# Retention and a gated MLP in one kernel: float32 scores from paired q and k, the state in 64x64 corners of the array, one pinned burst

## The chip, the cores and the metric

The kernel runs on one core of one Trainium2 chip. The metric is device time of one execution in microseconds. Its engines are named as in the profile: PE is TensorE (matmul), PEld its weight loads, DVE is VectorE, ACT is ScalarE, POOL is GpSimd, SP issues the DMAs. SBUF is the working memory; PE writes to PSUM, eight banks of 2 KB per partition, which DVE and ACT read.

## The reference

Inputs are q, k and v of shape (8, 8, 576, 64): batch B, head H, position S, head width D. First comes a retention layer per head, then a gated MLP with a spatial gate, per batch.

```python
scores = scale * np.matmul(q, k.transpose(0, 1, 3, 2))      # scale = 1/sqrt(D)
gamma = 1.0 - 2.0 ** (-5.0 - np.arange(H))
Dmat = np.where(rel >= 0, gamma[:, None, None] ** rel[None], 0.0)   # rel = pos_row - pos_col
attn = np.matmul(scores * Dmat[None], v)
x = attn.transpose(0, 2, 1, 3).reshape(B, S, H * D)          # (8, 576, 512)
h = np.maximum(x @ w_in, 0.0)                                # w_in is float64, 512 x 1024
u, v = h[..., :512], h[..., 512:]
v_n = (v - mean(v)) / np.sqrt(var(v) + 1e-06)                # over the last axis
v_s = np.einsum('ts,bsd->btd', w_spatial, v_n) + b_spatial[None, :, None]
out = (u * v_s) @ w_out                                      # w_out is float64, 512 x 512
```

## The kernel before

**Retention** works in chunks of 128 positions, four and a tail of 64 per batch (`NC`, `TL`). Inside a chunk the masked scores are formed directly. What earlier chunks contribute comes from a state of 64x64 per head: `state(c)` adds kᵀv of the chunk to the decayed state, `outp(c)` multiplies the state with the decayed q (`qsc`, line 283) and adds the masked scores times v (line 286). The sum `xo` is split into a rounded high part and a low remainder (lines 290, 291), because the MLP's matmuls run in float32r, three to a product (`mm3`, lines 316 to 318).

Two heads share the 128 partitions in most tiles: head 2p on rows 0 to 63, head 2p+1 on rows 64 to 127. The state is kept block-diagonal, 128x128 per pair of heads, and the blocks off the diagonal are zero.

**Scores** exist in two forms. Batch 0 (`DIRECT = 1`) uses `scores_direct`: float32 matmuls of depth 64, even heads on the upper half of the array's rows and odd heads on the lower half. Batches 1 to 7 use `split_qk` and `scores`: q and k come twice over the partitions (`qk`), ACT and DVE split them into high and low parts (lines 225 to 228), one float32r matmul of depth 128 per head and 256 columns gives two partial sums (line 241), ACT copies one out (243), DVE adds the other (244) and POOL applies the mask (245). `prep(c)` scales k by `kd` (256) and q by `qs` (259) on POOL.

**The MLP** of a batch is `v_block` (five, one per chunk), then in `main` eight `u` tiles, eight `vs` tiles (the spatial gate) and eight `f` tiles (the output), each followed by its work on ACT and DVE. Batch 0's v blocks are traced beside its retention; later v blocks are in `main`.

**What sets the order.** The code is traced in one order and a planner reorders it, by the traced order as priority and by simulated times; afterwards each engine runs its list in order, with semaphore waits. `interleave` mixes `main(b)` with `retention(b + 1)`: each `yield` carries a weight, and whichever side is behind its share (`ta`, `tr`) is traced next. `keep_in_program_order` ties an instruction to the one traced just before it on the same engine; before the change only the DMAs of the start are tied so. `issue_after` holds the conversion of w_spatial and w_out behind a mark. At the start the float64 weights are converted with integer arithmetic on DVE (`from_f64`, lines 166 to 170 and 160), eight quarters of w_in (`w_half`), then w_out (`w_o`). The loads of `qk` lie in a pool `late`, which is opened where the weights' staging pool `sp` was.

**PSUM**: two banks for scores (`ps_sc`), one each for `ds` and `xo` (`ps_x`), four for the MLP (`ps_m`).

Of the kernel before, what the change touches and what calls it, by code (L numbers as in the profile page):

```python
# [10 lines left out]
F32 = mybir.dt.float32  # L11
# [21 lines left out]
DIRECT = 1  # L33
# [3 lines left out]
def retention_gmlp(ctx, tc, kvq, kp, qk, qk_t, qp_t, kp_t, v_t, w_in, w_sp, b_sp, w_out, amask, qscale, kdec, sdec, out):  # L37
# [10 lines left out]
    am = cp.tile([P, H, C], F32, name="am")  # L48
# [12 lines left out]
    st = [cp.tile([P, NP, P], F32, name=f"st{i}") for i in range(3)]  # L61
    late = []
# [9 lines left out]
    low = cp.tile([P, 1], F32, name="low")  # L72
    nc.vector.memset(low[:D], 0.0)
    nc.vector.memset(low[D:], -1.0)

# [14 lines left out]
    def load_k(b, c):  # L90
        n = C if c < NC else TL
        if b < DIRECT:
            t = wk.tile([P, NP, C], F32, name=f"kp_{b}_{c}", tag="ks")
            dma(t[:, :, :n], kp[b, c] if c < NC else kp_t[b])
            return t, None
        t = late[0].tile([P, 2, H, C], F32, name=f"qk_{b}_{c}", tag="qk", bufs=2)
        dma(t[:, :, :, :n], qk[b, c] if c < NC else qk_t[b])
        return t[:, 0], t[:, 1]

    def load_v(b, c):  # L100
        t = ld.tile([P, 3, 512], F32, name=f"kvq_{b}_{c}", tag="kvq")
        qp = t[:, 0].rearrange("p (a n) -> p a n", a=NP)
        if c < NC:
            dma(t, kvq[b, c])
        else:
            dma(qp[:, :, :TL], qp_t[b])
            dma(t[:TL, 2], v_t[b])
        return qp, t[:, 1], t[:, 2]

    def load(b, c):  # L110
        chunk[b, c] = load_k(b, c) + load_v(b, c)
# [30 lines left out]
    k00 = load_k(0, 0)  # L142
    v00 = load_v(0, 0)
    chunk[0, 0] = k00 + v00
    dma(am, amask)
# [4 lines left out]
    k01 = load_k(0, 1)  # L150
    fetch_win(1, 2)
    chunk[0, 1] = k01 + load_v(0, 1)
    fetch_win(1, 3)
    for t in st:
        nc.gpsimd.memset(t, 0.0)
# [23 lines left out]
    def w_o():  # L179
        for db in range(NDB):  # L180
            from_f64(wout[0][:, db], wout[1][:, db], staged["o", db], wk.tile([P, DM], F32, name=f"f_o{db}", tag="ks"))
# [13 lines left out]

    def retention(b, then=None):
        at = {}
        qsc = {}
        ready = {}

        def scores_direct(c):
            n = C if c < NC else TL
            k, _, q, _, _ = chunk[b, c]
            ps = [ps_sc.tile([P, 4, C], F32, name=f"sc_{b}_{c}_{i}", tag="sc") for i in range(2)]
            for h in range(H):
                i, p = h % 2, h // 2
                r = slice(i * D, (i + 1) * D)
                nc.tensor.matmul(ps[i][:n, p, :n], k[r, p, :n], q[r, p, :n], start=True, stop=True)
                if h == 3:
                    yield 0.9  # L210
            a = [wk.tile([P, 4, C], F32, name=f"at_{b}_{c}_{i}", tag="at", bufs=4) for i in range(2)]
            for i in range(2):
                nc.vector.tensor_tensor(out=a[i][:n, :, :n], in0=ps[i][:n, :, :n], in1=am[:n, i::2, :n], op=ALU.mult)
            at[c] = [a[h % 2][:, h // 2] for h in range(H)]
            yield 0.9

        def split_qk(c):
            n = C if c < NC else TL
            q, k, _, _, _ = chunk[b, c]
            ready[c] = []  # L220
            for hf in range(2):
                qh = wk.tile([P, 4, 2, C], F32R, name=f"qh_{b}_{c}_{hf}", tag="qh")
                ks = wk.tile([P, 4, C], F32R, name=f"ks_{b}_{c}_{hf}", tag="ks")
                hs = slice(4 * hf, 4 * hf + 4)
                nc.scalar.copy(out=ks[:, :, :n], in_=k[:, hs, :n])  # L225
                nc.vector.scalar_tensor_tensor(out=ks[:, :, :n], in0=ks[:, :, :n].bitcast(F32), scalar=low, in1=k[:, hs, :n], op0=ALU.mult, op1=ALU.add)  # L226
                nc.scalar.copy(out=qh[:, :, 0, :n], in_=q[:, hs, :n])
                nc.vector.tensor_tensor(out=qh[:, :, 1, :n], in0=q[:, hs, :n], in1=qh[:, :, 0, :n].bitcast(F32), op=ALU.subtract)  # L228
                ready[c].append((qh, ks))

        def scores(c):
            at[c] = []
            n = C if c < NC else TL
            for hf in range(2):
                qh, ks = ready[c][hf]
                hs = slice(4 * hf, 4 * hf + 4)
                a = wk.tile([P, 4, C], F32, name=f"at_{b}_{c}_{hf}", tag="at", bufs=4)
                for p in range(2):
                    ps = ps_sc.tile([P, 2, 2, C], F32, name=f"sc_{b}_{c}_{hf}_{p}", tag="sc")
                    for i in range(2):  # L240
                        nc.tensor.matmul(ps[:n, i, :, :n], ks[:, 2 * p + i, :n], qh[:, 2 * p + i, :, :n], start=True, stop=True)  # L241
                    t = late[0].tile([P, 2, C], F32, name=f"a2_{b}_{c}_{hf}_{p}", tag="a2", bufs=2)
                    nc.scalar.copy(out=t[:n, :, :n], in_=ps[:n, :, 1, :n])  # L243
                    nc.vector.tensor_tensor(out=a[:n, 2 * p:2 * p + 2, :n], in0=ps[:n, :, 0, :n], in1=t[:n, :, :n], op=ALU.add)  # L244
                nc.gpsimd.tensor_tensor(out=a[:n, :, :n], in0=a[:n, :, :n], in1=am[:n, hs, :n], op=ALU.mult)  # L245
                at[c] += [a[:, h] for h in range(4)]
                yield 0.48

        def prep(c):
            _, _, q, kn, _ = chunk[b, c]  # L250
            n = C if c < NC else TL
            if b >= DIRECT:
                split_qk(c)
# [8 lines left out]
        def state(c):  # L262
            _, _, _, kn, vv = chunk[b, c]
            ps = ps_x.tile([P, NP, D], F32, name=f"ds_{b}_{c}", tag="ds")
            for h in range(H):
                nc.tensor.matmul(ps[h % 2 * D:(h % 2 + 1) * D, h // 2, :], kn[:, h * D:(h + 1) * D], vv[:, h * D:(h + 1) * D], start=True, stop=True)  # L266
            new = st[(c + 1) % 2]
            for i in range(2):
                r = slice(i * D, (i + 1) * D)
                if c == 0:  # L270
                    nc.scalar.copy(out=new[r, :, r], in_=ps[r])
                else:
                    nc.vector.tensor_tensor(out=new[r, :, r], in0=ps[r], in1=st[2][r, :, r], op=ALU.add)
            if c + 1 < NC:
                nc.gpsimd.tensor_tensor(out=st[2], in0=new, in1=sd.broadcast_to([P, NP, P]), op=ALU.mult)

        def outp(c):
            n = C if c < NC else TL
            vv = chunk[b, c][4]
            ps = ps_x.tile([P, NP, C], F32, name=f"xo_{b}_{c}", tag="xo")  # L280
            if c > 0:
                for p in range(NP):
                    nc.tensor.matmul(ps[:, p, :n], st[c % 2][:, p, :], qsc[c][:, p, :n], start=(p == 0), stop=False)  # L283
            for h in range(H):
                p, i = h // 2, h % 2
                nc.tensor.matmul(ps[i * D:(i + 1) * D, p, :n], vv[:n, h * D:(h + 1) * D], at[c][h][:n, :n],  # L286
                                 start=(c == 0), stop=(c == 0 or p == NP - 1))
            t = slice(c * C, c * C + n)
            hi, lo = (xs[b][:, i, :, t] if c < NC else xt[:, :, i] for i in range(2))
            nc.scalar.copy(out=hi, in_=ps[:, :, :n])  # L290
            mark["x", b, c] = nc.vector.tensor_tensor(out=lo, in0=ps[:, :, :n], in1=hi.bitcast(F32), op=ALU.subtract).ins  # L291
# [5 lines left out]
        if b >= DIRECT:  # L297
            for c in range(2):
# [129 lines left out]
    for step, _ in enumerate(retention(0, more)):  # L428
        if step < 4:
            next(wv)  # L430
# [83 lines left out]
```

## Time and profile before

| | |
|---|---|
| median of three runs | 622.74 us (622.13 to 623.81) |
| the profiled execution, its own time | 622.56 us |
| its span, first to last instruction | 620.8 us |
| busy: PE, DVE, ACT, POOL | 594.9, 433.5, 311.2, 212.0 us |
| mean granted TensorE clock | 0.973 of full |
| moved by DMA | 80.25 MB, 129 GB/s on average |

How to read the rows that follow. A timeline row has the start in us from the span's start, the length in us, the engine, the line of the kernel, the operation, what it writes and reads, the tile of the array (rows*columns), the shapes and the number of records merged into the row; in brackets the idle time before it and what ended that. A group row has shapes and count, then busy us and the mean ns of one, then the engine's idle time before and its releaser. Busy time counts overlapping records once. A float32 matmul is recorded as two matmuls, a float32r one as a single one.

### The profile page before, as it was taken

The page shows a single profiled execution, that of the slowest core. Times are in us where ns is not written, and L with a number is a line of the kernel's source. Part 1 is how long each engine was busy: PE and PEld are TensorE (multiplying, and loading weights), DVE is VectorE, ACT ScalarE, POOL GpSimd, SP SyncE. Part 2 cuts the span into 40 slices and gives each one's busy share as a digit, 9 for nine tenths or more (in the row PEclk, how much of TensorE's full clock was granted, in tenths as well). Part 3 has the DMA queues.
Part 4 walks back from the last instruction along what each step waited for, and adds up shares of the span by engine and source line. Part 5 has one row for each costly group of instructions (what it writes and reads, how often), then busy time and mean ns, then how long its engine had stood idle before and what let it go on. Part 6 is the DMA issues. An engine that isn't in the chain of part 4 may idle for free.

```text
span 620.8 us, 11999 instructions
## 1 busy us (share of the span) xinstructions
PE 594.9 (96%) x4660; PEld 537.3 (87%) x4660; DVE 433.5 (70%) x865; ACT 311.2 (50%) x736; POOL 212.0 (34%) x174
## 2 busy tenths in 40 slices
PE   6977968999999999999999999999999999999997
PEld 4666957887999889997999889997899979998997
DVE  4998798769854796749965697747956598634440
ACT  2346564357633574346633585346733477234522
POOL 2524024526512544224532355214531345310000
PEclk8888977999999999999999999999999999999999
DMA  8735725473324435155324434155333533010002
GB/s 308 251 98 165 262 73 177 168 259 120 94 77 169 146 121 168 61 176 197 87 86 150 165 119 110 62 177 200 104 124 112 185 137 86 18 49 30 1 1 77
DMA packets 42971, 80.25 MB, mean 129 GB/s; under 512 B 22049, under 2 KB 32289, under 8 KB 39330
## 3 DMA queue, kind: packets, MB, share of 16 engines
q1 hardware_dynamic: 42914, 79.49, 38.2%
q8 instruction: 36, 0.59, 0.4%
q14 instruction: 21, 0.17, 0.1%
HBM read 70.03 MB, written 9.44 MB: 128 GB/s over the span
## 4 chain that ended last, share of the span: by engine, by line
PE 86%; DVE 7%; DMA 3%; issue 1%; ACT 1%; SPq 0%; POOL 0%; ACTq 0%; DVEq 0%; POOLq 0%
PE xo L286 6%; PE f L316 6%; PE vs L316 6%; PE u L316 6%; PE f L318 5%; PE f L317 5%; PE vs L317 5%; PE vs L318 5%; PE sc L241 5%; PE v L316 5%; PE u L317 5%; PE u L318 5%; PE v L318 5%; PE v L317 4%; PE xo L283 4%; PE ds L266 3%
## 5 line engine op out<-in xcount | busy, mean ns | idle before, releaser
L245 POOL TENSOR_TENSOR at<-at,am 128x512 f32<-128x512 f32 (+1 forms) x70 | 100.3, 1433 | 122.1 <-DVE at L244 120.4
L228 DVE TENSOR_TENSOR qh<-qk,qh 128x512 fp32r<-128x512 f32 (+1 forms) x70 | 94.1, 1344 | 0.0
L244 DVE TENSOR_TENSOR at<-sc,a 128x256 f32<-128x256 f32 (+1 forms) x140 | 49.9, 388 | 59.9 <-ACT a L243 59.0
L256 POOL TENSOR_TENSOR kvq<-kvq,kd 128x512 f32<-128x512 f32 x32 | 37.2, 1164 | 141.2 <-DMA kvq<-in_kvq 115.8
L316 PE MATMUL u<-x,win 128*128 128x288 f32 x256 | 79.2, 309 | 0.0
L316 PE MATMUL f<-g,wout 128*128 128x288 f32 x256 | 77.7, 303 | 0.0
L316 PE MATMUL vs<-wsp,vn 128*128 128x288 f32 x256 | 77.4, 302 | 0.0
L317 PE MATMUL vs<-wsp,vn 128*128 128x288 f32 x256 | 75.9, 297 | 0.0
L317 PE MATMUL u<-x,win 128*128 128x288 f32 x256 | 75.9, 297 | 0.0
L318 PE MATMUL vs<-wsp,vn 128*128 128x288 f32 x256 | 75.9, 297 | 0.0
L318 PE MATMUL u<-x,win 128*128 128x288 f32 x256 | 75.8, 296 | 0.0
L386 ACT CAST g<-vs 128x288 fp32r<-128x288 f32 x64 | 25.4, 403 | 100.6 <-DVE vs L385 100.6
L317 PE MATMUL f<-g,wout 128*128 128x288 f32 x256 | 75.7, 296 | 0.0
L318 PE MATMUL f<-g,wout 128*128 128x288 f32 x256 | 75.7, 296 | 0.0
L226 DVE SCALAR_TENSOR_TENSOR ks<-ks,low,qk 128x512 fp32r<-128x512 f32 (+1 forms) x70 | 63.4, 905 | 3.0 <-ACT ks L225 2.2
L396 ACT COPY o<-f 128x288 f32<-128x288 f32 x64 | 25.6, 400 | 70.3 <-PE f L318 67.1
L318 PE MATMUL v<-win,x 128*128 128x512 f32 x128 | 52.5, 410 | 3.7 <-DVE x L291 3.7
L316 PE MATMUL v<-win,x 128*128 128x512 f32 x128 | 53.6, 420 | 2.1 <-ACT x L290 2.1
L243 ACT COPY a<-sc 128x256 f32<-128x256 f32 (+1 forms) x140 | 43.9, 356 | 18.5 <-PE sc L241 17.2
L259 POOL TENSOR_TENSOR qsc<-kvq,qs 128x512 f32<-128x512 f32 (+1 forms) x32 | 41.1, 1284 | 33.6 <-DMA kvq<-in_qp_t 33.6
L317 PE MATMUL v<-win,x 128*128 128x512 f32 x128 | 51.6, 403 | 0.0
L286 PE MATMUL xo<-at,kvq 128*64 128x128 f32 (+1 forms) x640 | 49.2, 281 | 2.5 <-POOL at L245 1.6
(92 smaller groups left out, 1407.3 us busy)
## 6 DMA issues: line engine op xcount, KB each, us to landing
qk<-in_qk SPq DMA_DIRECT2D x28, 1024.0 KB, 4.9
kvq<-in_kvq SPq DMA_DIRECT2D x32, 768.0 KB, 5.4
out<-o SPq DMA_DIRECT2D x64, 144.0 KB, 2.0
raw_i<-in_w_in SPq DMA_DIRECT2D x8, 512.0 KB, 5.5
qk<-in_qk_t SPq DMA_DIRECT2D x7, 512.0 KB, 4.5
raw_o<-in_w_out SPq DMA_DIRECT2D x4, 512.0 KB, 4.2
wl_s<-in_w_sp SPq DMA_DIRECT2D x4, 288.0 KB, 2.8
kp<-in_kp SPq DMA_DIRECT2D x4, 256.0 KB, 5.8
```

Of the source, the lines that this page charges most:

```text
L226: nc.vector.scalar_tensor_tensor(out=ks[:, :, :n], in0=ks[:, :, :n].bitcast(F32), scalar=low, in1=k[:, hs, :n], op0=ALU.mult, op1=ALU.add)
L228: nc.vector.tensor_tensor(out=qh[:, :, 1, :n], in0=q[:, hs, :n], in1=qh[:, :, 0, :n].bitcast(F32), op=ALU.subtract)
L241: nc.tensor.matmul(ps[:n, i, :, :n], ks[:, 2 * p + i, :n], qh[:, 2 * p + i, :, :n], start=True, stop=True)
L243: nc.scalar.copy(out=t[:n, :, :n], in_=ps[:n, :, 1, :n])
L244: nc.vector.tensor_tensor(out=a[:n, 2 * p:2 * p + 2, :n], in0=ps[:n, :, 0, :n], in1=t[:n, :, :n], op=ALU.add)
L245: nc.gpsimd.tensor_tensor(out=a[:n, :, :n], in0=a[:n, :, :n], in1=am[:n, hs, :n], op=ALU.mult)
L256: nc.gpsimd.tensor_tensor(out=kh, in0=kh, in1=kd.broadcast_to([P, H, D]), op=ALU.mult)
L259: nc.gpsimd.tensor_tensor(out=t[:, :, :n], in0=q[:, :, :n], in1=qs[:, :, :n], op=ALU.mult)
L286: nc.tensor.matmul(ps[i * D:(i + 1) * D, p, :n], vv[:n, h * D:(h + 1) * D], at[c][h][:n, :n], start=(c == 0), stop=(c == 0 or p == NP - 1))
L316: nc.tensor.matmul(ps, w[0], r[0], start=start, stop=False)
L317: nc.tensor.matmul(ps, w[0], r[1], start=False, stop=False)
L318: nc.tensor.matmul(ps, w[1], r[0], start=False, stop=stop)
```

## The change

All batches form their scores directly in float32 from paired q and k. One transfer per chunk, `qkv`, holds q and k as pairs of heads, k by position, and v (four times 512 values per partition); `qk`, `kp`, `qp_t`, `kp_t`, `split_qk`, the old `scores` and the pool `late` are gone, and the mask is one DVE multiplication of 128x1024 from PSUM.

`state` and `outp` become `burst`. For the state update each head's kᵀv is cut into two halves of 64 positions, so that 16 float32 matmuls of 64x64 go to the four corners of the array, into two banks (one per row half), and DVE adds the two banks and the decayed state in two steps. The state is held as 64x64 per head, with no zero blocks, and the decayed state's part of the output is 8 matmuls in the four corners. In odd pairs the heads swap column halves, which changes the order of x's features; the rows of w_in are permuted on the host to match. The values' matmuls keep depth 128 and 64 columns; in the tail they go to the corners as well.

The helper `mm` ties every retention matmul to the PE instruction traced before it. A chunk is now traced as: `prep(c + 1)`, the burst of c, the load of c + 2, then the scores of c + 1, with new weights for `yield` and `tr`. Scores and bursts share a PSUM tag of two tiles with two banks each. w_out's staging moves from the tag `qh` to the tag `raw` of the staging pool, the conversion's scratch likewise; there are four o buffers instead of three, and the weight conversion of w_in's v half is driven by two steps of two quarters instead of four steps of one.

```diff
-DIRECT = 1
...
-    ps_sc = ctx.enter_context(tc.tile_pool(name="ps_sc", bufs=2, space=PSUM))
-    ps_x = ctx.enter_context(tc.tile_pool(name="ps_x", bufs=1, space=PSUM))
+    ps_r = ctx.enter_context(tc.tile_pool(name="ps_r", bufs=2, space=PSUM))
...
-    st = [cp.tile([P, NP, P], F32, name=f"st{i}") for i in range(3)]
-    late = []
+    st = [cp.tile([P, NP, D], F32, name=f"st{i}") for i in range(3)]
...
+    def load(b, c):
+        t = ld.tile([P, 4, 512], F32, name=f"qkv_{b}_{c}", tag="qkv")
+        q, k = (t[:, i].rearrange("p (a n) -> p a n", a=NP) for i in range(2))
...
+        elif (b, c) == (0, 0):
+            dma(t[:, :2], qkv[b, c, :, :2])
+            dma(am, amask)
+            dma(t[:, 3], qkv[b, c, :, 3])
+            dma(t[:, 2], qkv[b, c, :, 2])
         else:
+            dma(t, qkv[b, c])
+        chunk[b, c] = q, k, t[:, 2], t[:, 3]
...
     def fetch_wout(db):
-        t = wk.tile([P, DM], U64, name=f"raw_o{db}", tag="qh")
+        t = sp.tile([P, DM], U64, name=f"raw_o{db}", tag="raw", bufs=3)
...
+    def mm(out, w, r, start, stop):
+        tc.keep_in_program_order(nc.tensor.matmul(out, w, r, start=start, stop=stop))
...
         def scores(c):
+            n = rows(c)
+            q, k, _, _ = chunk[b, c]
+            ps = ps_r.tile([P, 2, NP, C], F32, name=f"sc_{b}_{c}", tag="r")
+            for p in range(NP):
+                for i in range(2):
+                    mm(ps[:n, i, p, :n] if c < NC else ps[half[i], i, p, :n], k[half[i], p, :n], q[half[i], p, :n], True, True)
+            a = wk.tile([P, 2, NP, C], F32, name=f"at_{b}_{c}", tag="at")
+            if c < NC:
+                nc.vector.tensor_tensor(out=a, in0=ps, in1=am, op=ALU.mult)
...
+        def burst(c):
+            n = rows(c)
+            _, _, kn, vv = chunk[b, c]
+            ps = ps_r.tile([P, 2, 2, 2 * C], F32, name=f"ox_{b}_{c}", tag="r")
+            ds = ps[:, :, 0].rearrange("p r (a d) -> p r a d", a=NP)
+            xo = ps[:, :, 1].rearrange("p j (a n) -> p j a n", a=2)
+            if c < NC:
+                for p in range(NP):
+                    for r in range(2):
+                        for i in range(2):
+                            m = i ^ r
+                            hd = slice((2 * p + m) * D, (2 * p + m + 1) * D)
+                            mm(ds[half[m], r, p], kn[half[r], hd], vv[half[r], hd], True, True)
+            order = [(p, i) for j in range(2) for p, i in ((2 * j, 0), (2 * j, 1), (2 * j + 1, 1), (2 * j + 1, 0))]
+            if c > 0:
+                for p, i in order:
+                    mm(xo[half[i ^ (p % 2)], i, p // 2, :n], st[c % 2][half[i], p], qsc[c][half[i], p, :n], p < 2, False)
+            for p, i in order:
+                h = 2 * p + i
+                r = slice(0, n) if c < NC else half[i]
+                mm(xo[half[i ^ (p % 2)], i, p // 2, :n], vv[r, h * D:(h + 1) * D], at[c][r, i, p, :n], c == 0, c == 0 or p >= 2)
...
+            if c < NC:
+                new, tmp = st[(c + 1) % 2], st[2]
                 if c == 0:
+                    nc.scalar.copy(out=tmp, in_=ds[:, 0])
                 else:
+                    nc.vector.tensor_tensor(out=tmp, in0=ds[:, 0], in1=tmp, op=ALU.add)
+                nc.vector.tensor_tensor(out=new, in0=ds[:, 1], in1=tmp, op=ALU.add)
+                if c + 1 < NC:
+                    nc.gpsimd.tensor_tensor(out=tmp, in0=new, in1=sd.broadcast_to([P, NP, D]), op=ALU.mult)
+            nc.scalar.copy(out=hi, in_=src)
+            mark["x", b, c] = nc.vector.tensor_tensor(out=lo, in0=src, in1=hi.bitcast(F32), op=ALU.subtract).ins
...
         prep(0)
+        scores(0)
+        yield 0.95
         for c in range(NC + 1):
             if then:
                 then(c)
             if c < NC:
                 prep(c + 1)
+            burst(c)
+            if c + 2 < len(nxt) and nxt[c + 2][0] < B:
                 load(*nxt[c + 2])
+            yield 1.7
+            if c < NC:
+                scores(c + 1)
+                yield 0.95
...
-        if step < 4:
+        if step < 2:
+            next(wv)
             next(wv)
...
-        interleave(main(b, b == 0), retention(b + 1) if b + 1 < B else [], 50.0 if b else 38.0, 15.4)
+        interleave(main(b, b == 0), retention(b + 1) if b + 1 < B else [], 50.0 if b else 38.0, 12.5)
```

More of the change, by code (lines that the diff above doesn't have):

```diff
@@ L32, with retention_gmlp @@
 EPS = 1e-6
-DIRECT = 1
 @with_exitstack
-def retention_gmlp(ctx, tc, kvq, kp, qk, qk_t, qp_t, kp_t, v_t, w_in, w_sp, b_sp, w_out, amask, qscale, kdec, sdec, out):
+def retention_gmlp(ctx, tc, qkv, qk_t, v_t, w_in, w_sp, b_sp, w_out, amask, qscale, kdec, sdec, out):
     nc = tc.nc
@@ L88, in dma @@
             tc.keep_in_program_order(ins)
[L90 to L104, printed above, removed]
-        else:
[L106 to L111, printed above, removed]
+    def load(b, c):
+        t = ld.tile([P, 4, 512], F32, name=f"qkv_{b}_{c}", tag="qkv")
+        q, k = (t[:, i].rearrange("p (a n) -> p a n", a=NP) for i in range(2))
+        if c == NC:
+            dma(t[:, :2].rearrange("p i (a n) -> p i a n", a=NP)[:, :, :, :TL], qk_t[b])
+            for i in range(2):
+                dma(t[i * TL:(i + 1) * TL, 3], v_t[b])
+        elif (b, c) == (0, 0):
[3 more added lines that the diff above has]
+            dma(t[:, 2], qkv[b, c, :, 2])
+        else:
+            dma(t, qkv[b, c])
+        chunk[b, c] = q, k, t[:, 2], t[:, 3]
     staged = {}
@@ L141, in retention_gmlp @@
     fetch_win(1, 0)
[L142 to L145, printed above, removed]
+    load(0, 0)
     fetch_win(1, 1)
@@ L149, in retention_gmlp @@
     dma(sd, sdec)
-    k01 = load_k(0, 1)
     fetch_win(1, 2)
-    chunk[0, 1] = k01 + load_v(0, 1)
+    load(0, 1)
     fetch_win(1, 3)
-    for t in st:
-        nc.gpsimd.memset(t, 0.0)
     nc.gpsimd.memset(vt2.bitcast(F32), 1.0)
@@ L198, in retention @@
         qsc = {}
[L199 to L229, printed above, removed]
@@ L231, in scores @@
-        def scores(c):
[L232 to L247, printed above, removed]
+        half = [slice(i * D, (i + 1) * D) for i in range(2)]
@@ new lines, in rows @@
+        def rows(c):
+            return C if c < NC else TL
+        def scores(c):
+            n = rows(c)
[7 more added lines that the diff above has]
+                nc.vector.tensor_tensor(out=a, in0=ps, in1=am, op=ALU.mult)
+            else:
+                for i in range(2):
+                    r = half[i]
+                    nc.vector.tensor_tensor(out=a[r, i, :, :n], in0=ps[r, i, :, :n], in1=am[r, i, :, r], op=ALU.mult)
+            at[c] = a
@@ L260, in prep @@
                 qsc[c] = t
[L262 to L269, printed above, removed]
+        def burst(c):
+            n = rows(c)
+            _, _, kn, vv = chunk[b, c]
[5 more added lines that the diff above has]
+                    for r in range(2):
+                        for i in range(2):
+                            m = i ^ r
[9 more added lines that the diff above has]
+                mm(xo[half[i ^ (p % 2)], i, p // 2, :n], vv[r, h * D:(h + 1) * D], at[c][r, i, p, :n], c == 0, c == 0 or p >= 2)
+            t = slice(c * C, c * C + n)
+            hi, lo = ((xs[b][:, i, :, t] if c < NC else xt[:, :, i]).rearrange("p (a j) n -> p j a n", j=2) for i in range(2))
+            src = xo[:, :, :, :n]
+            if c < NC:
+                new, tmp = st[(c + 1) % 2], st[2]
@@ L270, in state @@
                 if c == 0:
-                    nc.scalar.copy(out=new[r, :, r], in_=ps[r])
+                    nc.scalar.copy(out=tmp, in_=ds[:, 0])
                 else:
[L273 to L291, printed above, removed]
@@ L296, in retention @@
         nxt = [(b, c) for c in range(NC + 1)] + [(b + 1, c) for c in range(2)]
-        if b >= DIRECT:
-            for c in range(2):
-                if (b, c) not in chunk:
-                    load(b, c)
         prep(0)
+        scores(0)
+        yield 0.95
         for c in range(NC + 1):
@@ L304, in retention @@
                 then(c)
-            yield from (scores_direct if b < DIRECT else scores)(c)
             if c < NC:
                 prep(c + 1)
-                state(c)
-                yield 0.85
-            outp(c)
-            if c + 2 < len(nxt) and nxt[c + 2][0] < B and (nxt[c + 2][0] == b or b >= DIRECT):
+            burst(c)
+            if c + 2 < len(nxt) and nxt[c + 2][0] < B:
                 load(*nxt[c + 2])
-            yield 2.0 if c else 1.0
+            yield 1.7
+            if c < NC:
+                scores(c + 1)
+                yield 0.95
     def mm3(ps, w, r, start, stop):
```

34 lines of the change are left out of this document (12 added, 22 removed).

## The prediction

> **What bounds the kernel now.** I read the page first: which engine is busy, and where the TensorE clock was granted (40 slices).
>
> ```profile
> span 620.8 us, 11999 instructions
> PE 594.9 (96%) x4660; PEld 537.3 (87%) x4660; DVE 433.5 (70%) x865; ACT 311.2 (50%) x736; POOL 212.0 (34%) x174
> PEclk8888977999999999999999999999999999999999
> ```
>
> TensorE (PE) is the bound, but not everywhere: the clock row is low in the first eighth, where other engines hold it up. So next the busy time by stage (columns: PE, PEld, DVE, ACT, POOL, clock, DMA share, GB/s).
>
> ```profile
> 8.70:59.40 50.70, 39.83 (x328) 30.74 (x329) 44.42 (x86) 22.14 (x42) 18.01 (x15) 0.85 0.60 198
> 80.00:100.00 20.00, 12.27 (x64) 9.64 (x63) 19.90 (x33) 12.08 (x27) 6.44 (x4) 0.62 0.39 145
> 136.80:208.40 71.60, 71.60 (x577) 65.12 (x576) 50.20 (x105) 38.06 (x93) 28.01 (x23) 1.00 0.40 134
> ```
>
> Up to 59.4 us VectorE (DVE) leads. From 80 to 100 us DVE has 19.90 of 20 us of work, and PE works 12.27 us at a clock of 0.62. Later PE is never idle. Because PE's records overlap (a 288-column matmul shows 0.30 us, yet the next starts 0.13 us later), I price PE work from start to start. The stage borders are in the PE timeline:
>
> ```profile
> 59.43 0.44 PE L316 MATMUL u<-x,win 128*128 128x288 f32 x1
> 133.50 0.40 PE L316 MATMUL v<-win,x 128*128 128x512 f32 x1
> 563.34 0.50 PE L316 MATMUL v<-win,x 128*128 128x512 f32 x1
> ...
> 563.91 0.39 PE L318 MATMUL v<-win,x 128*128 128x512 f32 x1
> 564.14 0.39 PE L316 MATMUL v<-win,x 128*128 128x512 f32 x1
> ...
> 616.72 0.29 PE L318 MATMUL f<-g,wout 128*128 128x288 f32 x1
> ```
>
> The last batch runs without retention beside it: 563.34 to 616.85, 53.5 us. Batches 1 to 6, each with the next one's retention, take (563.34-133.50)/6 = 71.64 us. So **one retention costs PE 18.1 us**. Batch 0's u, vs and f (53.5 less 13.1 for its 56 v matmuls of 0.234: 40.4) with the first retention ought to take 58.5 us; they take 133.50-59.43 = 74.07. The 15.6 us over are the hole at 80 to 100 us.
>
> **What the parts cost now.** Retention's pieces in the PE timeline, each with the row after it:
>
> ```profile
> 252.41 0.63 PE L241 MATMUL sc<-qh,ks 128*128 128x256 f32 x4
> 252.88 0.30 PE L316 MATMUL vs<-wsp,vn 128*128 128x288 f32 x1
> ...
> 254.61 0.30 PE L384 MATMUL vs<-wtl,vt 66*128 66x288 f32 x1
> 254.84 0.69 PE L266 MATMUL ds<-kvq 128*64 128x64 f32 x16
> 255.46 0.74 PE L241 MATMUL sc<-qh,ks 128*128 128x256 f32 x4
> 256.03 0.29 PE L316 MATMUL vs<-wsp,vn 128*128 128x288 f32 x1
> ...
> 259.78 1.06 PE L283 MATMUL xo<-qsc,st 128*128 128x128 f32 x8
> 260.76 1.09 PE L286 MATMUL xo<-at,kvq 128*64 128x128 f32 x16
> 261.79 0.40 PE L316 MATMUL f<-g,wout 128*128 128x288 f32 x1
> 262.02 0.29 PE L317 MATMUL f<-g,wout 128*128 128x288 f32 x1
> 262.15 0.29 PE L318 MATMUL f<-g,wout 128*128 128x288 f32 x1
> ```
>
> A float32 matmul is two records here (ds: 8 matmuls, x16). Scores: 0.47 per four, 0.93 per chunk, in the whole array. A change of array shape costs on both sides: the matmul before ds is followed after 0.23 instead of 0.13 (+0.10), the four scores behind ds take 0.57 instead of 0.47 (+0.10), f's first is followed after 0.23 (+0.10). State update: 0.10+0.62+0.10 = 0.82. Decayed state (L283): 0.98, eight records of 0.11 and the switch. Values (L286): 1.03+0.10 = 1.13. A middle chunk: 0.93+0.82+0.98+1.13 = 3.86; chunk 0, without L283 but with the switch in (0.10): 2.98. The 64-row tail:
>
> ```profile
> 51.63 1.00 PE L283 MATMUL xo<-qsc,st 128*128 128x64 f32 x8
> 52.56 0.68 PE L286 MATMUL xo<-at,kvq 64*64 64x64 f32 x16
> 53.17 0.69 PE L266 MATMUL ds<-kvq 128*64 128x64 f32 x16
> ```
>
> 0.93 for the state, 0.61+0.2 for the values, as much for its scores: 2.55. Sum 2.98+3x3.86+2.55 = 17.1. The 1.0 us short of 18.1 I put down to pieces that the planner scatters, each with two more switches.
>
> **What they cost after.** Paired scores exist in batch 0 (L208):
>
> ```profile
> 24.75 0.40 PE L318 MATMUL v<-win,x 128*128 128x512 f32 x1
> 25.08 1.16 PE L208 MATMUL sc<-kvq,kp 64*128 64x128 f32 x16
> 26.17 0.45 PE L266 MATMUL ds<-kvq 128*64 128x64 f32 x6
> ...
> 45.06 0.68 PE L208 MATMUL sc<-kvq,kp 64*64 64x64 f32 x8
> ```
>
> 1.09 with the switch out, +0.10 in, +0.10 on the next matmul: 1.29 against 0.93. **The scores lose 0.36 us a chunk on PE**; what they save is elsewhere. The other row is a warning: eight records of 64 columns fill 0.68, as long as L286's sixteen of the same size above. The planner had put four matmuls of one corner in a row, so none overlapped. The pinned order prevents that.
>
> The state update becomes 16 matmuls of half the depth, 32 records. Where four corners run at once these are 8 rounds, as many as the 8 pairs now: 0.52 inside, 0.10 to enter: 0.62, with no exit, since the decayed state follows in the same shape. Its 8 matmuls at four corners are 4 rounds of 0.11: 0.44 instead of 0.98. Then one switch and the values, 0.10+1.13. Burst: 0.62+0.44+1.23 = 2.29. Middle chunk 1.29+2.29 = 3.58; chunk 0 3.14; tail 0.81 for scores and, with state and values both in four corners (0.23 each) and one entry and exit (0.35), 0.81 more: 1.62. Sum 3.14+3x3.58+1.62 = 15.5, and 0.3 for remaining scatter, as the pin leaves less: **15.8 instead of 18.1**.
>
> Four corners at once is shown by no row; rows show two, in columns (L266) and in rows (L208). Bounds: as taken, or only two at a time: ds +0.46 a chunk, state +0.44, tail +0.46, 19.4 in all. I take the first, as both directions overlap separately.
>
> The Trainium skill has a rule against it. "TensorE: Matmul & The Clock Gate", section "Wait — 56ns, not 53.3ns?", says that starts are never closer than about 25 ns however small the matmul. By that, an estimate from this page, ds would take 0.80 instead of 0.46, the tail 0.34 more, a retention 17.5, and the kernel 612. The same page, section "Measured speedup vs the span model", puts about 4 ns between the starts of different tiles; the following row decides for single starts only.
>
> ```profile
> 27.22 0.28 PE L266 MATMUL ds<-kvq 128*64 128x64 f32 x2
> ```
>
> Two records of 0.27 fill 0.28, so starts 0.01 apart do occur; a lasting rate above ds's (16 in 0.46, 29 ns) is untested here.
>
> **DVE, ACT, POOL.** Per retention, the split of q and k and the adding and masking go:
>
> ```profile
> L245 POOL TENSOR_TENSOR at<-at,am 128x512 f32<-128x512 f32 (+1 forms) x70 | 100.3, 1433 | 122.1 <-DVE at L244 120.4
> L228 DVE TENSOR_TENSOR qh<-qk,qh 128x512 fp32r<-128x512 f32 (+1 forms) x70 | 94.1, 1344 | 0.0
> L244 DVE TENSOR_TENSOR at<-sc,a 128x256 f32<-128x256 f32 (+1 forms) x140 | 49.9, 388 | 59.9 <-ACT a L243 59.0
> L226 DVE SCALAR_TENSOR_TENSOR ks<-ks,low,qk 128x512 fp32r<-128x512 f32 (+1 forms) x70 | 63.4, 905 | 3.0 <-ACT ks L225 2.2
> L213 DVE TENSOR_TENSOR at<-sc,am 128x512 f32<-128x512 f32 x8 | 5.2, 681 | 1.4 <-PE sc L208 1.4
> ```
>
> DVE loses (94.1+63.4+49.9)/7 = 29.6 us a batch and gains four masks of 2x0.68 and a small tail, about 6: 50 becomes 27 of about 69 us. In the steady stage this is worth nothing in itself: PE hides it. In the hole at 80 to 100 us it is the cause: the splits stand in DVE's queue ahead of what PE waits for. With them gone I let 2.5 of the 15.6 us stand, for the conversion of w_out. That one is fetched later, through slots that wsp leaves; some 30 us of u and vs cover it. The transfers of a chunk, one in place of two, and one more o buffer lie under PE too.
>
> **The start.** Here the change takes something. The pin puts each score group behind whatever PE instruction was traced before it, so in batch 0 scores(1) must follow all of v_block(0), which waits for the fourth converted quarter of w_in and now ends here:
>
> ```profile
> 18.36 1.95 PE L208 MATMUL sc<-kvq,kp 64*128 64x128 f32 x16
> ...
> 28.09 0.50 PE L318 MATMUL v<-win,x 128*128 128x512 f32 x1 [0.31 <-DVE x L291]
> ```
>
> Scores(1), at 18.36 now, cannot start before 28.4. Then each chunk is a chain that ends in the evacuation:
>
> ```profile
> L290 ACT CAST x<-xo 128x512 fp32r<-128x512 f32 x32 | 18.8, 586 | 11.9 <-PE xo L286 11.9
> L291 DVE TENSOR_TENSOR x<-xo,x 128x512 fp32r<-128x512 f32 x32 | 21.9, 683 | 9.8 <-ACT x L290 9.5
> ```
>
> Scores 1.2, mask 1.4, burst 2.3, evacuation 2.1 (0.6, 0.7 and two adds of half the size, 0.4 each as an estimate), v block 12x0.234 = 2.8: 9.8 us, three times; tail 5.4 (scores, mask, burst 0.8 each, copy and subtraction 1.1, v block 1.9); 2.5 for DVE's queue. u starts at 28.4+29.4+5.4+2.5 = 66 instead of 59.4. Bounds: 59.4, where DVE's 44.42 us remain the limit, and 76, were each of four waits 2.5 us longer.
>
> **Sum** (us, in the profiled execution): 66 to u; batch 0, 40.4+15.8+2.5 = 58.7; six batches of 53.5+15.8 = 69.3, 415.8; the last batch and the end as now, 620.8-563.34 = 57.5. Span 598.0; the profiled run's own time is 622.56 for 620.8, so +1.8: **600 us**. That run is 0.18 below the median of 622.74. A difference under 0.3% (1.9 us) counts as no change.
>
> **The rivals.**
> *Rate limit:* records start no faster than the fastest lasting rate seen, 29 ns. ds +0.46 a chunk, tail +0.46, retention 18.1, and 600+7x2.3 = 616. For: nothing faster is in the trace. Against: that rate is also just the 64 columns' own time. 0.2.
> *Only two corners at once* (retention 19.4): 600+7x3.6 = 625, the other side of the line. It decides from 18.9 per retention up (600+7x3.1 = 622). For: the serial tail scores at 45.06; against: that was one corner repeated. 0.1.
> *The burst waits for its mask:* the sequence is fixed, so where `at` is late PE stands. With some 3.8 us of main work between scores and burst, and a mask of 1.4, DVE must be more than 2.4 us behind. From 0.8 us per burst (28 of them, 22 us) the gain is gone; at 1.2 the time is 634. DVE's fall to 27 us speaks against. 0.06.
> *The hole stays:* 13 us of it return because the w_out conversion alone holds DVE: 613. Its 11 us lie in 59 to 85, before f. 0.1.
> *The pairs don't form as written* because main matmuls get between: +0.35 per break, 28 bursts, 610. 0.04.
>
> The forecast has the remaining 0.5. **Range** 588 (u at 59.4, no rests) to 617, which takes in the rate limit and leaves out two corners, the late mask and ends below. Faster: everything but the 0.1, the 0.06 and some of the longest starts, 0.84; same 0.07; slower 0.09.
>
> **What would show it.** Starts of the ds records: 32 in about 0.5 us for four corners, 0.9 for a limit. Distance of v's first matmuls: 69.3. u's first start near 66, scores(1) directly behind v_block(0). No DVE stage at 80 to 100 us. DVE near 40% busy in the steady stage. I am wrong if retention still costs 18, or if PE shows idle time ahead of the values.

## The result, and the profile after

The changed kernel takes **605.17 us** (median of 4 runs, 603.30 to 606.82), where the kernel before takes 622.68 beside it (622.13 to 623.81). The ratio is 0.9716, with a 95% interval of 0.9684 to 0.9748: 2.8% faster. The forecast was 600.0, with a range of 588 to 617. One slow run, 697.17 us at a granted clock of 0.744 in the experiment with the copy ahead, is left out of that kernel's median below, which is 597.69 us without it and 599.95 with it.

First the span, the busy times and the granted clock of the changed kernel, from its page.

```profile
span 602.6 us, 13266 instructions
PE 569.0 (94%) x5708; PEld 513.0 (85%) x5708; DVE 286.9 (48%) x629; ACT 208.7 (35%) x448; POOL 93.9 (16%) x101
PEclk9587799999999999999999999999999999999999
```

DVE is down from 433.5 to 286.9 us. The low clock still fills the first eighth, so the start still isn't PE's own. Busy times by stage show the same (columns: PE, PEld, DVE, ACT, POOL, clock, DMA share, GB/s).

```profile
9.50:71.00 61.50, 39.87 (x393) 29.69 (x394) 43.01 (x84) 21.41 (x39) 13.22 (x12) 0.69 0.40 136
80.00:110.00 30.00, 24.63 (x299) 22.49 (x298) 23.80 (x40) 10.24 (x23) 11.00 (x9) 1.00 0.38 129
133.80:202.60 68.80, 68.80 (x714) 62.59 (x712) 30.73 (x70) 23.71 (x52) 11.58 (x13) 1.00 0.27 87
```

Before u, PE is busy as long as before (39.87 us against 39.83), but in 61.5 us instead of 50.7, at a clock of 0.69 instead of 0.85. In the steady stage PE is never idle, and DVE has fallen from 50.20 us in 71.6 to 30.73 in 68.8 (27 was forecast). The stage borders stand in the PE timeline.

```profile
70.98 0.30 PE L271 MATMUL u<-x,win 128*128 128x288 f32 x1
...
133.81 0.50 PE L271 MATMUL v<-win,x 128*128 128x512 f32 x1
...
545.77 0.39 PE L271 MATMUL v<-win,x 128*128 128x512 f32 x1
```

Against the terms of the forecast (us):

| stage | before | forecast | measured |
|---|---|---|---|
| to u of batch 0 | 59.43 | 66 | 70.98 |
| from u to v of batch 1 | 74.07 | 58.7 | 62.83 |
| batches 1 to 6, each | 71.64 | 69.3 | 68.66 |
| the last batch and the end | 57.5 | 57.5 | 56.8 |
| span | 620.8 | 598.0 | 602.6 |

Batch 1's v starts at 133.81, where it started at 133.50 before. What the first two stages won from the hole they lost at the start. The whole gain, 6x(71.64-68.66) = 17.9 us, is in the steady stage. There a burst looks like this (batch 3's retention, with vs matmuls of batch 2 on both sides):

```profile
249.79 0.30 PE L339 MATMUL vs<-wtl,vt 66*128 66x288 f32 x1
250.02 0.69 PE L177 MATMUL ox<-qkv 64*64 64x64 f32 x32
250.53 0.62 PE L177 MATMUL ox<-qsc,st 64*64 64x128 f32 x16
251.08 1.09 PE L177 MATMUL ox<-at,qkv 128*64 128x128 f32 x16
252.10 0.40 PE L271 MATMUL vs<-wsp,vn 128*128 128x288 f32 x1
```

From start to start: state update 0.51 for 32 records, decayed state 0.55, values 1.02. With 0.10 to enter (249.79 to 250.02 is 0.23 in place of 0.13) and 0.10 on the next matmul, the burst costs 2.28. 2.29 was forecast.

What holds up the first 134 us is in the table of PE's waits (us in total, times, longest). For the line L247 that leads it, ACT's copy of x, the second view has what ended ACT's idle time before it over the whole run (us, times).

```profile
PE v L271 <- ACT x L247: 14.7, 4, 6.0
PE ox L177 <- DVE at L196: 5.3, 4, 2.3
PE ox L177 <- POOL qkv L208: 4.1, 1, 4.1
PE ox L177 <- DVE x L248: 1.9, 1, 1.9
```

```profile
  DVE st L244: 39.1, 19
```

Chunk 3 of batch 0 shows it in order of time, on PE, DVE and ACT:

```profile
53.81 1.09 PE L177 MATMUL ox<-at,qkv 128*64 128x128 f32 x16 [0.67 <-DVE at L196]
56.51 0.42 DVE L244 TENSOR_TENSOR st<-ox,st 128x256 f32<-128x256 f32 x1
57.02 0.59 ACT L247 CAST x<-ox 128x512 fp32r<-128x512 f32 x1 [1.66 <-DVE st L244]
57.66 0.80 PE L271 MATMUL v<-win,x 128*128 128x512 f32 x1 [2.75 <-ACT x L247]
58.25 0.63 PE L272 MATMUL v<-win,x 128*128 128x512 f32 x1
58.68 0.63 PE L273 MATMUL v<-win,x 128*128 128x512 f32 x1
...
63.08 0.96 PE L177 MATMUL sc<-qkv 64*64 64x64 f32 x14
```

The v block waits for the evacuation, and ACT's copy out of PSUM does not start when the burst ends (54.9) but when DVE has done the state's second add (L244). The forecast had both adds in its chain, but not the time that they spend in DVE's queue behind other work. Of the 39.1 us only 9.3, in 7 waits, lie in the first 134 us; in the steady stage PE is not idle for it. In the kernel before, the copy (L290) waited for PE. State and output now lie in the two halves of the same PSUM banks, and the state's adds are traced ahead of the copy.

The rows show a second loss. Behind the wait the v block's matmuls start 0.43 us apart, where they start 0.23 apart in the steady stage, and the granted clock is 0.50 from 57.6 to 63.1 us. It is 0.50 as well behind the waits of 2.35 and 3.62 us for the copy in chunks 1 and 2 (33.6 to 36.3 and 46.0 to 50.0 us).

### The profile page after: what moved, and what is told of

Read it like the earlier page. It is cut to its first block, busy times and chain, and to the rows that moved or that the text cites. A ratio compares the mean times of both kernels' runs of the same rounds, so it can differ in the third digit from the quotient of the medians.

```text
span 602.6 us, 13266 instructions
## 1 busy us (share of the span) xinstructions
PE 569.0 (94%) x5708; PEld 513.0 (85%) x5708; DVE 286.9 (48%) x629; ACT 208.7 (35%) x448; POOL 93.9 (16%) x101
## 4 chain that ended last, share of the span: by engine, by line
PE 84%; DVE 8%; DMA 4%; ACT 2%; issue 1%; SPq 0%; ACTq 0%; DVEq 0%
PE ox L177 9%; PE f L271 6%; PE vs L271 6%; PE f L272 6%; PE f L273 6%; PE v L271 5%; PE sc L177 5%; PE u L271 5%; PE vs L273 5%; PE vs L272 5%; PE v L272 5%; PE u L272 5%; PE v L273 5%; PE u L273 5%; PE v L287 2%; DMA raw_o<-in_w_out 2%
## 5 line engine op out<-in xcount | busy, mean ns | idle before, releaser
L271 PE MATMUL u<-x,win 128*128 128x288 f32 x256 | 77.1, 301 | 0.0
L272 PE MATMUL u<-x,win 128*128 128x288 f32 x256 | 75.6, 295 | 0.0
L273 PE MATMUL u<-x,win 128*128 128x288 f32 x256 | 75.2, 294 | 0.0
L196 DVE TENSOR_TENSOR at<-sc,am 128x1024 f32<-128x1024 f32 x32 | 38.8, 1213 | 73.0 <-PE sc L177 73.0
L271 PE MATMUL v<-win,x 128*128 128x512 f32 x128 | 55.8, 436 | 14.9 <-ACT x L247 14.7
L208 POOL TENSOR_TENSOR qkv<-qkv,kd 128x512 f32<-128x512 f32 x32 | 34.2, 1069 | 177.9 <-DMA qkv<-in_qkv 123.6
L272 PE MATMUL v<-win,x 128*128 128x512 f32 x128 | 53.8, 420 | 0.0
L273 PE MATMUL v<-win,x 128*128 128x512 f32 x128 | 53.6, 419 | 0.0
L271 PEld LDWEIGHTS vs<-wsp,vn 128*128 128x128 f32 x256 | 48.1, 188 | 3.4 <-issue 2.4
L271 PEld LDWEIGHTS u<-x,win 128*128 128x128 f32 x256 | 48.0, 188 | 2.6 <-issue 1.2
L271 PEld LDWEIGHTS f<-g,wout 128*128 128x128 f32 x256 | 48.0, 188 | 1.1 <-issue 0.2
L272 PEld LDWEIGHTS u<-x,win 128*128 128x128 f32 x256 | 48.1, 188 | 0.4
L272 PEld LDWEIGHTS vs<-wsp,vn 128*128 128x128 f32 x256 | 48.2, 188 | 0.0
L273 PEld LDWEIGHTS f<-g,wout 128*128 128x128 f32 x256 | 48.1, 188 | 0.0
```

The costliest lines, as they stand in the source:

```text
L196: nc.vector.tensor_tensor(out=a, in0=ps, in1=am, op=ALU.mult)
L271: nc.tensor.matmul(ps, w[0], r[0], start=start, stop=False)
L272: nc.tensor.matmul(ps, w[0], r[1], start=False, stop=False)
L273: nc.tensor.matmul(ps, w[1], r[0], start=False, stop=stop)
```

## The experiments

The theory after the result has three parts: the pin costs most of the start; the copy behind the state's adds costs the rest; and the remains of the hole are DVE's conversion of w_out, held up by staging tiles that it shares. A rival for the start is DVE itself, which has 43 to 44 us of work before u in either kernel and would then hold u near 70 whatever the order.

**The pin, loosened and taken away.** In the first kernel each retention matmul is tied only to the retention matmul before it; in the second to nothing.

```diff
-        tc.keep_in_program_order(nc.tensor.matmul(out, w, r, start=start, stop=stop))
...
+        with tc.issue_after(last[0]):
+            last[0] = nc.tensor.matmul(out, w, r, start=start, stop=stop).ins
```

> Edit: each retention matmul is tied to the retention matmul before it, not to the PE instruction traced last; all else as in the changed kernel (605.2 us). Theory A: the late start of u (70.98 us) is the price of that tie, since scores(1) stands behind all of v_block(0). Then scores(1) starts near 15 instead of 26.6, u near 62, and the time is about 597 us; the period of 68.8 us of the later batches stays. Rival B: the start is set by what a burst's evacuation and DVE's queue wait for, whatever the order on PE: u stays within 2 us of 71, the time within 2 us of 605.

```diff
-        tc.keep_in_program_order(nc.tensor.matmul(out, w, r, start=start, stop=stop))
+        nc.tensor.matmul(out, w, r, start=start, stop=stop)
```

> Edit: the tie is left out altogether; all else as in the changed kernel (605.2 us). My prediction had the tie prevent scattered pieces (1.0 us per retention before). Theory: in the later batches each group of retention matmuls is one batch of equal tiles whose inputs are there together, so the planner keeps it whole anyway; the period stays 68.8, only the start changes, as with the tie to the last retention matmul: u near 62, time about 592 us. Rival: without a tie the pieces scatter or corners repeat, the period rises by 1 us or more: 599 us or more.

Tied among themselves: 592.44 us, 0.9489 of the kernel before (0.9454 to 0.9525), with u at 62.09. Free: 589.65, 0.9466 (0.9439 to 0.9493). The PE timeline of the free one:

```profile
15.79 2.08 PE L177 MATMUL sc<-qkv 64*128 64x128 f32 x16 [0.17 <-DMA qkv<-in_qkv]
...
59.16 0.30 PE L271 MATMUL u<-x,win 128*128 128x288 f32 x1
...
119.00 0.50 PE L271 MATMUL v<-win,x 128*128 128x512 f32 x1
...
186.77 1.16 PE L177 MATMUL sc<-qkv 64*128 64x128 f32 x16
...
530.94 0.39 PE L271 MATMUL v<-win,x 128*128 128x512 f32 x1
```

Scores(1) of batch 0 starts at 15.79; in the changed kernel it stands at 26.58, behind v_block(0):

```profile
26.58 2.08 PE L177 MATMUL sc<-qkv 64*128 64x128 f32 x16
```

u starts 11.8 us earlier, v of batch 1 14.8 us. The rival falls: DVE's work before u is much the same (40.43 us from 9.5 us on, against 43.01), and u starts at 59. The period is (530.94-119.00)/6 = 68.66, exactly that of the pinned kernel, and the score group at 186.77 is in one piece, as all retention groups from 119 us on are. So the pin does nothing for the steady stage, and its 15 us are all cost. The wait for the copy is still there, but smaller (7.8 us in 3 waits instead of 14.7 in 4). The clock has a part in the gain: the same 393 PE records before u are busy for 36.44 us at a granted clock of 0.79, against 39.87 at 0.69.

**The copy ahead of the state's adds.** Only the order of tracing changes: L247 and L248 move ahead of the `if c < NC:` block of the state.

```diff
+            nc.scalar.copy(out=hi, in_=src)
+            mark["x", b, c] = nc.vector.tensor_tensor(out=lo, in0=src, in1=hi.bitcast(F32), op=ALU.subtract).ins
             if c < NC:
                 new, tmp = st[(c + 1) % 2], st[2]
...
-            nc.scalar.copy(out=hi, in_=src)
-            mark["x", b, c] = nc.vector.tensor_tensor(out=lo, in0=src, in1=hi.bitcast(F32), op=ALU.subtract).ins
```

> Edit: after a burst, x's high and low part are traced before the state's two adds. Theory C: in the changed kernel ACT's copy of x waits for the state's add on DVE (39 us in 19 waits), because both read the same PSUM banks, and v blocks 0 to 3 stand behind that copy (PE waits of 14.7 us). Then those waits shrink to some 5 us, u starts near 63 instead of 71 and the time is about 598 us. Rival D: DVE's queue is late with the subtraction anyway, and the v block needs both parts: u within 2 us of 71, time 603 to 607.

597.69 us (597.68 to 602.21), 0.9608 (0.9567 to 0.9649): 7.5 us less than the changed kernel. Its waits, PE's and then ACT's, and u's first start:

```profile
PE v L271 <- ACT x L238: 3.7, 4, 1.4
PE ox L177 <- DVE at L196: 7.0, 5, 2.8
...
ACT x L238 <- PE ox L177: 19.2, 15, 1.7
```

```profile
66.72 0.45 PE L271 MATMUL u<-x,win 128*128 128x288 f32 x1
```

The copy now waits for PE's burst and no longer for DVE, and PE waits 3.7 us for it instead of 14.7. u is 4.3 us earlier, where 8 were expected: PE now waits longer for the masks (7.0 us instead of 5.3) and 2.8 us for DVE's part of x. The wait for the copy came from the order of the reads; that a shared bank is what makes the order binding was not tried alone.

**Corners in another order.** What the four corners are worth: the same matmuls, with only two corners in neighbouring instructions (for the decayed state the order becomes 0, 1, 4, 5, 2, 3, 6, 7).

```diff
-                for p in range(NP):
-                    for r in range(2):
+                for r in range(2):
+                    for p in range(NP):
...
-                for p, i in order:
+                for p, i in [order[s] for s in (0, 1, 4, 5, 2, 3, 6, 7)]:
```

> Edit: the same 64x64 matmuls in another order, so that neighbours use two corners instead of four (state update: all pairs of the upper row half, then of the lower; decayed state: twice the same two corners in a row). Theory: the order decides how many corners run at once. Then the 32 records of a state update take about 0.95 us instead of 0.49, the 16 of the decayed state 0.88 instead of 0.45; a retention costs 0.46x4+0.43x3+0.2 = 3.3 us more, the period goes from 68.8 to 72.1, the time to about 628 us. Rival: PE's queue runs ahead and finds free corners by itself: 605 us.

614.22 us, 0.9857 (0.9820 to 0.9895), between the two expectations. The state update of a chunk 0, in the changed kernel and then in this one, where a middle chunk's state update and decayed state follow:

```profile
208.45 0.69 PE L177 MATMUL ox<-qkv 64*64 64x64 f32 x32
209.07 1.09 PE L177 MATMUL ox<-at,qkv 128*64 128x128 f32 x16
```

```profile
205.78 0.50 PE L271 MATMUL v<-win,x 128*128 128x512 f32 x1
...
211.57 0.97 PE L177 MATMUL ox<-qkv 64*64 64x64 f32 x32
212.47 1.09 PE L177 MATMUL ox<-at,qkv 128*64 128x128 f32 x16
...
224.01 0.80 PE L177 MATMUL ox<-qkv 64*64 64x64 f32 x26
224.60 0.32 PE L177 MATMUL ox<-qsc,st 64*64 64x128 f32 x1
224.64 0.28 PE L177 MATMUL ox<-qkv 64*64 64x64 f32 x4
...
486.40 0.50 PE L271 MATMUL v<-win,x 128*128 128x512 f32 x1
```

0.90 us in place of 0.62, +0.28; two corners at a time would be +0.46. In the middle chunk a record of the decayed state starts at 224.60, before the last records of the state update, which the tied order puts ahead of it. So PE runs some matmuls of free corners ahead of waiting ones, but not all: the order in the program counts. State update and decayed state together take 1.40 us there (the values start at 225.41) in place of 1.06. The period becomes (486.40-205.78)/4 = 70.16, 1.5 more than in the changed kernel; 0.28 and three times 0.34 are 1.3 of it.

**The w_out staging with tiles of its own.** In the changed kernel raw_o shares the tag `raw` with the staging of w_in and w_sp.

```diff
-        t = sp.tile([P, DM], U64, name=f"raw_o{db}", tag="raw", bufs=3)
+        t = sp.tile([P, DM], U64, name=f"raw_o{db}", tag="rawo", bufs=2)
```

> Edit: w_out's raw tiles get a tag of their own with two buffers, instead of the three that w_in, w_spatial and b_spatial pass through; all else as in the changed kernel (605.2 us). Theory: the later conversion of w_out (its DVE work runs to 103 us, before the change to 85) makes bursts of batch 1 wait for their masks in DVE's queue (5.4 us of waits between 80 and 106 us); with an earlier load u to the next v shrinks from 62.8 to about 58 us, the time to 601. Rival: the loads are held by SP's order, not by the buffers, or PE's loss there has other causes: within 1.5 us of 605.

603.59 us, 0.9679 (0.9657 to 0.9702), which is not apart from the changed kernel's 605.17. u starts at 69.87 and v of batch 1 at 132.88, 63.0 us later, where 62.83 were. The staging tiles don't make the hole; this part of the theory falls. But the edit hardly moved the conversion: the first loads of raw_o go out at 71.85 instead of 72.64, behind those of w_sp in SP's queue, and the conversion starts on DVE at 80.6 instead of 80.8. So it does not test what the conversion itself costs.

**The direct scores alone.** The kernel before, with its own direct path (L208) for all batches, unpinned, and with its old state and output parts.

```diff
-DIRECT = 1
+DIRECT = 8
...
-    late.append(ctx.enter_context(tc.tile_pool(name="late", bufs=2)))
```

> Edit: the kernel before with its own direct scores in all batches (DIRECT = 8), its state, values and planner's order as they were, nothing pinned: the scores' part of the change alone. Theory: DVE's load falls, but PE pays 0.36 us more per chunk, and about 0.9 where the planner puts four matmuls of one row half in a row (chunk 1 and some tails): period 71.6 to about 74; the hole at 80 to 100 us closes (11 us less from u to the next batch's v): 622.7+6x2.4-11 = 626 us. Rival: the scores are what made the kernel faster: about 605 us, period near 69.

630.46 us, 1.0108 (1.0087 to 1.0129): 1.1% slower. Its stage borders:

```profile
59.25 0.44 PE L313 MATMUL u<-x,win 128*128 128x288 f32 x1
129.50 0.50 PE L313 MATMUL v<-win,x 128*128 128x512 f32 x1
...
568.90 0.50 PE L313 MATMUL v<-win,x 128*128 128x512 f32 x1
```

The period is (568.90-129.50)/6 = 73.23, 1.6 above the 71.64 before, which is what 0.36 us a chunk and a dearer tail come to. From u to v are 70.25 us against 74.07. A retention costs 1.6 more there too, so the hole shrank by some 5.4 us of its 15.6. DVE's relief by itself does not close it (11 us were expected), and PE's loss in six batches is larger.

**Scores right behind the burst.** The two groups are traced with nothing between them, under the pin of the change.

```diff
-            yield 1.7
             if c < NC:
                 scores(c + 1)
-                yield 0.95
+            yield 2.65 if c < NC else 1.7
```

> Edit: the scores of c+1 are traced right behind the burst of c, with one yield for both; the tie is as in the changed kernel. Theory A again, by another road: scores(1) then stand before v_block(0) although tied, start near 15 instead of 26.6, and u starts near 62 (605-9 = 596 us). Besides, one exit from the small tiles and one entry go per chunk, about 0.2 us, 0.8 per retention: the period falls from 68.8 to 68.0, 5 us more: 591 us. Rival: with the evacuation behind 1.1 us more of PE work and two PSUM tiles busy, the steady stage loses what it gains: period 68.8 or above, time 596 or more.

```profile
65.56 0.30 PE L270 MATMUL u<-x,win 128*128 128x288 f32 x1
127.91 0.50 PE L270 MATMUL v<-win,x 128*128 128x512 f32 x1
...
468.04 0.50 PE L270 MATMUL v<-win,x 128*128 128x512 f32 x1
```

593.29 us, 0.9511 (0.9481 to 0.9542). Two gains: the period is (468.04-127.91)/5 = 68.03, 0.63 less, since each chunk leaves the small tiles once instead of twice; and u starts 5.4 us earlier (9 were expected), because scores(c + 1) is now traced ahead of the v block and not behind it. The second is the pin's cost seen a third way.

**Both repairs of the start.** The chain of the first experiment and the order of the third.

> Edit: both earlier edits together, the tie to the last retention matmul (592.4 us alone) and x evacuated before the state's adds (599.9 us alone). If they take different waits: u starts near 59 and the time is about 588 us. If both take the same wait, or DVE's work of the start is the next bound (44 us of DVE before u, as in the kernel before): u at 60 to 62, time 590 to 593.

592.07 us, 0.9492 (0.9461 to 0.9523): no better than the chain alone (592.44). u starts earlier (57.64), v of batch 1 does not (121.7, after 121.50). Something else is late by then. One of the waits is new against the changed kernel, for the first scores of batch 1:

```profile
PE sc L183 <- DMA qkv<-in_qkv: 3.5, 2, 3.3
```

Its chunk is loaded by the queue of SP, which stands on the load of w_sp; that in turn waits for staging tiles to come free:

```profile
39.27 17.43 SPq L79 DMA_DIRECT2D wl_s<-in_w_sp  x4
...
59.21 0.37 SPq L79 DMA_DIRECT2D qkv<-in_qkv  x1
```

**All together, and then the loads in another order.** The next kernel has the chain, the copy first, the adjacent groups and the staging tiles of w_out. The one after it issues the loads of w_sp and w_out after both chunk loads of batch 1 (they were started at chunks 3 and 4 of batch 0). The last one also loads `kd` second, ahead of the first chunk, for POOL's first scaling of k.

> Edit: the tie to the last retention matmul, x before the state's adds, scores right behind the burst, and w_out's raw tiles with their own buffers. If the parts add up: u near 60, u to the next v 57, period 68.0, together about 582 us. If the start is bound by DVE by now, 586 or more with the period still at 68.0.

```diff
-        elif c == 3:
-            fetch_wsp()
-        elif c == 4:
-            fetch_wout(0)
-            fetch_wout(1)
...
             vb += 1
+    fetch_wsp()
+    fetch_wout(0)
+    fetch_wout(1)
     with tc.issue_after(mark["x", 0, NC]):
```

> Edit: as the fastest so far (583.3 us: tie to the last retention matmul, x first, scores behind the burst, own tiles for w_out), and w_spatial's and w_out's loads are issued behind both chunk loads of batch 1 instead of ahead of them. Theory: SP stands at w_spatial's fourth load until the buffer is free, and batch 1's first scores wait for their chunk (3.1 us on PE); with the chunk loads ahead the wait goes, u to the next v from 62 to about 59: 580 us. Rival: w_spatial lands later and vs waits instead, or another wait takes the place: within 1.5 us of 583.

```diff
     fetch_win(1, 0)
+    dma(kd, kdec)
     load(0, 0)
     fetch_win(1, 1)
-    dma(kd, kdec)
```

> Edit: as the run above, and the small load of kd is issued second instead of sixth. Theory: the first burst waits 3.7 us for POOL's scaling of k, and that for kd, which lands behind 2.5 MB of larger loads; early, u starts some 2 us sooner, the time falls by 2 us against the run above. Rival: the fourth quarter of w_in sets v_block(0) and so u: no difference over 1 us.

| kernel | us | ratio to before | u | v of batch 1 |
|---|---|---|---|---|
| all together | 583.28 | 0.9355 (0.9326 to 0.9383) | 57.04 | 119.14 |
| and w_sp, w_out later | 580.74 | 0.9310 (0.9294 to 0.9326) | 57.95 | 115.40 |
| and kd second | 581.76 | 0.9328 (0.9312 to 0.9344) | 59.69 | 116.9 |

With the loads moved, u to v takes 115.40-57.95 = 57.45 us instead of 62.1. The medians differ by 2.5 us; the two profiled runs, from which the borders are read, by 3.9. The rows: the stage borders, and the chunk loads ahead of w_sp.

```profile
57.95 0.30 PE L276 MATMUL u<-x,win 128*128 128x288 f32 x1
115.40 0.50 PE L276 MATMUL v<-win,x 128*128 128x512 f32 x1
...
522.37 0.40 PE L276 MATMUL v<-win,x 128*128 128x512 f32 x1
```

```profile
49.01 6.13 SPq L79 DMA_DIRECT2D qkv<-in_qkv  x2
55.23 7.83 SPq L79 DMA_DIRECT2D wl_s<-in_w_sp  x4
```

The period is (522.37-115.40)/6 = 67.83. The wait for the masks is no longer among PE's first seven, and the hole is gone but for some 2.7 us (40.4 and a retention of 14.3 are 54.7 of the 57.45). What is left of PE's waits is led by 4.0 us of the first burst for POOL's scaling of k. `kd` brings nothing: these 4.0 us become 0.8, and the first scores wait 2.9 us for their own chunk instead.

The kernel with the loads moved is the best that was run: **580.74 us** (580.35 to 581.11), 6.9% below the kernel before.

## Why the prediction came out as it did

**The burst and the retention: right.** 2.29 us were forecast for the burst, 2.28 were measured; the two switches of the score groups were paid as taken from L208. The period was 69.3 forecast and 68.66 measured. With the prediction's own 53.5 for the main work a retention costs 15.2 instead of 15.8, and the 0.3 for scatter was not needed. (The last batch's own work on PE takes 53.4 here; the 0.7 less in the last stage lies mostly behind its last matmul.)

**Four corners: right, where two rivals were against it.** 32 records in 0.51 us are 16 ns each, half of the fastest lasting spacing that the trace of before had (29 ns). The limit of 29 ns and the two corners at a time both fall; the period, 68.66, leaves room for neither (each would add 2.3 to 3.6 us). By an estimate from the Trainium skill, "TensorE: Matmul & The Clock Gate", section "Wait — 56ns, not 53.3ns?", which has starts at least some 25 ns apart, the state update would take 0.80; the trace disagrees, with 0.51.

**The scores' loss: right.** +0.36 us a chunk was forecast, and the direct scores alone lengthen the period by 1.6. So the gain comes from the rest, 73.23 to 68.66: burst and corners. That is by subtraction; they were not run without the direct scores. The order of the corners alone was run, and is 1.5 of these 4.6.

**"u starts at 66": 5 us too small.** The term that failed is the price of the v blocks, "12x0.234 = 2.8". That spacing belongs to stages where PE is never idle. Here the three v blocks of the chain take 4.3, 4.9 and 5.4 us, most of it at 0.43 us a matmul and a granted clock of 0.50, and the tail's takes 3.4 instead of 1.9: 7.7 us more in all. The rest of the way from scores(1) to u takes 26.4 us, where 27.0 were forecast, and scores(1) starts at 26.58, 1.8 sooner than the prediction held possible. The wait for the copy is inside these 26.4: behind the bursts PE waits 2.35, 3.62 and 2.75 us instead of 2.1 each. The two adds were in the forecast's evacuation, but not the work that DVE does before and between them; these 2.4 us are about the 2.5 that were set aside for DVE's queue.

The slow clock stands behind PE's waits in each of these chunks, and where the waits shrink the clock rises (0.79 before u without the pin). That the waits bring it on fits the rows, but no run changed one without the other. So u at 66.72 with the copy first meets the forecast by chance: two of the chain's three v blocks still have half or more of their matmuls 0.43 us apart there (33.83 to 38.24 and 45.45 to 51.11 us). Without the pin u starts at 59.16, near the prediction's lower bound of 59.4, and in later kernels at 57.04, so DVE's work was no limit at 59.4.

**"Of the hole 2.5 us stand": almost 5 us too small.** A period of 68.66 leaves 15.2 for a retention; 40.4+15.2 = 55.6 of the 62.83 is work, so some 7 are left. Waits account for 5.3 of them: 3.4 for masks (the other 1.9 of the table's 5.3 fall before u) and 1.9 for DVE's part of x. What the remaining 2 us are is open. The cause that the prediction gave, w_out's conversion, is neither shown nor excluded: its steps stand in DVE's queue from 80.8 to 103.6 us, ahead of both masks and of the part of x that PE waits for, and tiles of its own hardly moved them. With other repairs in place the order of SP's loads turned out to hold this stage, 4.7 us of it. How much of the 7 us in the changed kernel was the loads alone was not run.

**"The pinned order prevents that": wrong in this kernel.** The prediction took from the scattered row at 45.06 that groups need pinning, and wrote 0.3 us of remaining scatter to a retention. Without any tie the period is the same 68.66; main matmuls get into the groups in batch 0 alone. What keeps the later groups whole was not tested; that a group's inputs and its one PSUM tile come free at once, so that all its matmuls are ready together, is only a likely reason.

The total missed by 4.6 us of span (602.6 against 598.0): +5.0 and +4.1 in the first two stages, -3.8 and -0.7 in the others. That it missed by so little is partly luck, since 9.1 too much and 4.5 too little stand against each other. The sign and the range held because the steady stage, which counts six times, was priced from start to start in rows of the trace; its four-corner rate stood in no row and was a judgement that held.

## What to carry to other kernels

Price a fixed order by what it puts in front of an instruction in the stage where inputs arrive one by one: a tie that is free in the steady stage cost 15 us in the first two stages here, and each tie should be tried without before it is kept. When two results move into one PSUM tile, look at who reads first: the reader that the next matmul waits for has to be traced first. And when one wait is repaired, look at the queue behind it before adding gains up: here two repairs of 13 and 7 us gave 13 together, and more came only with the other orders. Last, price a matmul at the clock of its own stage: the v blocks cost up to twice their steady price where PE had waited before them.

## What was not expected of the hardware

Matmuls of 64x64 in four corners keep up 16 ns per record over 32 records, where two halves kept up 29: cutting the state update's matmuls to half their depth costs no time inside the group on PE (32 records in 0.51 us, 16 in 0.52 before) as long as neighbouring instructions are in different corners. With two corners in neighbouring instructions the same 32 records took 0.28 us more, not 0.46, and a later matmul's record started at 224.60, ahead of earlier ones: PE reaches past a waiting corner, but only some way.
